# A planner that may hold a transpose back, and power-of-two scales in three vector operations

## The chip, the cores and the metric

The kernel runs on one core of one Trainium2 chip. The metric is the device time of one execution in microseconds (us), from its start to its end. Three executions of the kernel before took 875.47, 883.95 and 887.24 us, so the median is 883.95. A fourth one was profiled, and all rows below are from it.

The engines of the core are TensorE (PE in the rows, PEld for its loading of weights), VectorE (DVE), ScalarE (ACT), GpSimd (POOL) and SyncE (SP), which issues the transfers. Each engine works through its instructions strictly in the order in which the program lists them, and waits on semaphores for the others.

## The reference

Block-sparse attention over q, k and v of 4 batches x 8 heads x 768 rows x 64, followed by a feed-forward layer with a rational activation:

```
mask = |block_i - block_j| <= 1, or block 0 or 23 on either side, or a sampled block (3 for each row block)
attn = softmax(q k^T / 8 where mask) v
x    = attn as 3072 x 512
h    = x @ w_in                                  # 512 x 2048
g    = (a0 + a1 h + a2 h^2 + a3 h^3) / (1 + |b0| |h| + |b1| h^2 + 1e-6)
out  = g @ w_out                                 # 2048 x 512
```

The weights arrive as 64-bit floats and are unpacked on the chip. q, k, x and w_in are scaled by a power of two and split into two 16-bit parts (a high and a low one), so that products of 16-bit matmuls add up to 32-bit precision.

## The kernel before, in words

**Tiling.** The 3072 rows are twelve chunks of 256. A chunk needs eight row blocks of attention (`attention`, one for each batch and block of 32 rows; blocks 0 and 23 have three parts, the others one), which run through scores (L911), maxima (L921), exponentials (L939), a transpose of the probabilities (`turn`, L980), values (L1037); four blocks share one weighting (`weigh`, L1071) and one transpose of x (`turn_x`, L1109), whose result is split into xh (ACT, L150) and xl (DVE, L1125). The feed-forward layer then runs as eight units for each chunk (`unit`): two `into` pieces of 12 matmuls on TensorE (L1179 to L1181), the rational function in three ACT and seven DVE steps besides a logarithm and an exponential, and two `out` pieces of 6 matmuls (L1235 to L1237) into an accumulator.

**Preparation.** For each batch, k is read once for its range (ACT sums absolute values, `bound`, L400) and, after its scale is known, read again, split, transposed on TensorE (`rest`, L683) and written to DRAM. q is loaded by tiles of 128 rows (`prep_q`, L728, into the one buffer ldq), split into hlq (GpSimd high part, L154; DVE low part, L394), transposed (L758), copied by ACT (L762) and swapped by two transfers (L766, L767). Batches 0 and 1 find a scale for each q tile, batches 2 and 3 one for the batch.

**Scales.** `scales` (L343) makes a power of two from a maximum: a transpose on TensorE (`most`, L351) spreads the 128 partition maxima, DVE reduces them (L356), and four short DVE instructions on one column follow: a floor (L359), the exponent by a bit mask (L363), and the scale and its inverse (L367, L368). It is called 27 times: 12 for q tiles (scq), 2 for q batches (scqb), 8 for k and v (sc), 4 for w_in (scw) and once for the x of the first chunk (scx). `prep_q` makes from two inverses the softmax factor c and its negative in three DVE instructions (L746, L749, L752), 14 times.

**Order.** Nothing is ordered by hand. Each step is an `Op` with an engine, a price in ns, its predecessors and a priority. `issue` runs through a clock of its own: for each engine it takes the Op with the smallest key, which is the later of "engine free" and "inputs ready less a slack of 21 ns", then the priority; it writes that Op's instructions and books price and hand-over times (`LAT`). The result is a fixed order on each engine. Up to 80 us of the planner's clock it also writes idle-time matmuls on TensorE (`fill`, L162), whose result nobody uses.

Of the kernel before, what the change touches and what calls it, by code (L numbers as in the profile page):

```python
# [11 lines left out]
F32 = mybir.dt.float32  # L12
# [11 lines left out]
def kernel(  # L24
# [71 lines left out]
    VE, SC, PO, TE, SY = "DVE", "Activation", "Pool", "PE", "SP"  # L96
    LAT = {(SC, TE): 410, (VE, TE): 240, (PO, TE): 225, (TE, SC): 200, (TE, VE): 200, (TE, SY): 170, (VE, SC): 130, (VE, PO): 130,
# [19 lines left out]
    class Op:  # L117


        def __init__(self, eng, price, run, after=(), prio=0.0, takes=(), uses=(), unit=None, behind=None):  # L120
# [3 lines left out]
            self.after, self.behind = [a for a in after if a is not None], behind  # L124
# [3 lines left out]
            self.next, self.at, self.work = [], dict.fromkeys(self.engs, 0.0), 1.0  # L128
# [35 lines left out]
    def issue(ahead):  # L164
# [29 lines left out]
        while left:  # L194
            best = None
            for e, l in todo.items():
                for o in l:
# [7 lines left out]
                    key = (max(t - slack, now[e]) + (0 if e == o.engs[0] else other[e]), o.prio, o.n)  # L205
# [90 lines left out]
    coef = const.tile([P, 4], F32, name="coef")  # L296
    bias = const.tile([P, NB, NS], F32, name="bias")
# [6 lines left out]
    def setup():  # L304
# [5 lines left out]
        nc.vector.memset(coef[:, 0:1], 1.0)  # L310
        nc.vector.tensor_copy(out=coef[:, 1:2], in_=absb[:, 0:1])
# [31 lines left out]
    def scales(get, name, after, prio, slot=(), finish=None, keep=None):  # L343
# [14 lines left out]
        def floor():  # L358
            nc.vector.tensor_scalar(out=res[0][:, 0:1], in0=res[0][:, 0:1], scalar1=2.0 ** -100, scalar2=None, op0=ALU.max)  # L359

        def exponent():
            mi = res[0].bitcast(I32)
            nc.vector.tensor_scalar(out=mi[:, 1:2], in0=mi[:, 0:1], scalar1=0x7F800000, scalar2=None, op0=ALU.bitwise_and)  # L363

        def power():
            m, mi = res[0], res[0].bitcast(I32)
            nc.vector.tensor_scalar(out=mi[:, 2:3], in0=mi[:, 1:2], scalar1=-1.0, scalar2=float((2 * 127 + 14) << 23), op0=ALU.mult, op1=ALU.add)  # L367
            nc.vector.tensor_scalar(out=mi[:, 3:4], in0=mi[:, 1:2], scalar1=float(14 << 23), scalar2=None, op0=ALU.subtract)  # L368
            res[:] = [m[:, 2:3], m[:, 3:4]]
            if keep:  # L370
                keep(*res)
# [4 lines left out]
        a = Op(TE, 109, most, after, prio, takes=[s_ps])  # L376
        a = Op(VE, 260, largest, [a], prio, takes=slot, uses=[s_ps])
        return row(VE, [(69, floor), (69, exponent), (138, power)] + ([(138, final)] if finish else []), [a], prio, uses=slot), res
# [177 lines left out]
    def prep(b, when, what):  # L556
# [11 lines left out]
        for w in what:  # L568
# [40 lines left out]
            if w == 2:  # L609
# [4 lines left out]
                q_scale[b] = scales(lambda mx=mx: mx[0][:, 6:7], "scqb", [o], when(w, 0, n - 1))  # L614
                continue

            def largest(mx=mx, w=w):
# [5 lines left out]
                           finish=out_scale if w and b < PLAIN else None)  # L623
# [14 lines left out]
    def rest(b, w, j, d, o_scale, sc, prio, before):  # L638
# [60 lines left out]
        o = Op(TE, 445, transposes, [o], prio, takes=[s_ps], uses=[s_hl])  # L699
# [13 lines left out]
    def prep_q(b, t, prio, before):  # L713
# [57 lines left out]
        if own:  # L771
            o = Op(SC, 613, most, [o_ld], prio, uses=[s_ld])
            o, sc = scales(lambda: d["mx"][:, 0:1], "scq", [o], prio, sl_sc)
# [634 lines left out]
```

## Time and profile before

| | |
|---|---|
| median of three executions | 883.95 us |
| profiled execution | 879.92 us, its span from first to last instruction 878.2 us |
| TensorE busy | 827.3 us (94%), idle 51 us |
| VectorE busy | 725.5 us (83%) |
| ScalarE busy | 675.9 us (77%) |
| GpSimd busy | 112.3 us (13%) |
| transfers | 151 MB, 16 engines 66% busy |

A busy share is an average over stretches that differ, so the rows below go stretch by stretch. In a row of a group the columns are: line, engine, operation, what it writes and reads, count, total busy time, mean ns of one, then the idle time of the engine just before and what ended it. [...]

### The profile page before, as it was taken

The numbers are of one execution on the slowest core, as the hardware profiler recorded it, in microseconds if no ns is written. First come the engines' busy times: TensorE is split into PE (matmuls) and PEld (weight loads), VectorE is DVE, ScalarE is ACT, GpSimd is POOL, SyncE is SP. The second block draws the span as 40 slices with busy tenths as digits, with TensorE's granted clock in tenths as the row PEclk, the third lists the DMA queues.
The fourth block names the chain that finished last, engine by engine and source line by source line (L and its number), as shares of the span: only waits on it lengthen the run. The fifth ranks groups of instructions, "written<-read, shape, count | busy, mean of one in ns | idle before, by whom it ended". The sixth has DMA issues, their size and how long they took to land.

```text
span 878.2 us, 28042 instructions
## 1 busy us (share of the span) xinstructions
PE 827.3 (94%) x10338; PEld 642.6 (73%) x10338; DVE 725.5 (83%) x1746; ACT 675.9 (77%) x1450; POOL 112.3 (13%) x117
## 2 busy tenths in 40 slices
PE   8989868779899899999999999999999899999997
PEld 4456756657678687778878787778778788778886
DVE  6778998999998787787878686888888688778886
ACT  5789988987787788897777687897767587767563
POOL 1146426164300000100000000100000000000000
PEclk9999988998999999999999999999999999999999
DMA  8697799868656966888556956889545965740000
GB/s 195 154 215 224 209 206 202 217 205 215 140 152 169 282 156 175 216 241 229 140 147 177 250 164 172 216 222 242 147 137 160 235 159 155 179 108 26 1 26 24
DMA packets 240216, 151.22 MB, mean 172 GB/s; under 512 B 16208, under 2 KB 222928, under 8 KB 240080
## 3 DMA queue, kind: packets, MB, share of 16 engines
q1 hardware_dynamic: 240080, 149.43, 65.7%
q8 instruction: 82, 1.34, 0.7%
q14 instruction: 54, 0.44, 0.2%
HBM read 132.07 MB, written 11.01 MB: 163 GB/s over the span
## 4 chain that ended last, share of the span: by engine, by line
PE 62%; DVE 11%; DMA 9%; SPq 7%; ACT 6%; issue 3%; POOL 1%; ACTq 0%; POOLq 0%; DVEq 0%
PE acc L1235 8%; PE ph L1179 8%; PE acc L1236 8%; PE acc L1237 8%; PE ph L1180 7%; PE ph L1181 7%; PE av L1037 5%; PE sp L911 4%; PE pt L980 4%; DMA ldq<-in_q_dram 2%; DMA wl<-in_moe_w_in_dram 2%; SPq L1007 1%; DMA vg<-in_v_dram 1%; DMA ld<-in_v_dram 1%; DVE pr L921 1%
## 5 line engine op out<-in xcount | busy, mean ns | idle before, releaser
L1179 PE MATMUL ph<-xh,wi 128*128 128x256 f16 x768 | 214.1, 279 | 4.7 <-DVE tt L1196 3.6
L1181 PE MATMUL ph<-xh,wi 128*128 128x256 f16 x768 | 212.5, 277 | 2.2 <-POOL wi L514 2.2
L1180 PE MATMUL ph<-xl,wi 128*128 128x256 f16 x768 | 212.6, 277 | 0.1
L1235 PE MATMUL acc<-wo_h,gh 128*128 128x512 f32 x376 | 160.8, 428 | 0.0
L1237 PE MATMUL acc<-wo_h,gl 128*128 128x512 f32 x376 | 149.4, 397 | 3.3 <-DVE gl L1224 3.3
L1236 PE MATMUL acc<-wo_l,gh 128*128 128x512 f32 x376 | 149.4, 397 | 0.0
L1203 DVE SCALAR_TENSOR_TENSOR ab<-sq,absb,ab 128x512 f32<-128x512 f32 x96 | 73.4, 764 | 53.4 <-ACT ab L1200 53.3
L1186 ACT ACTIVATE sq<-ph,fc 128x512 f32<-128x512 f32 x96 | 65.8, 685 | 65.9 <-PE ph L1181 65.5
L1179 PEld LDWEIGHTS <-wi 128*128 128x128 f16 x768 | 76.3, 99 | 34.5 <-issue 17.4
L921 DVE CUSTOM_DVE_ANT_1 pr<-sp,bias 128x256 f32<-128x256 f32 x224 | 84.8, 418 | 10.1 <-PE sp L911 10.0
L1214 DVE SCALAR_TENSOR_TENSOR gh<-tt,par,rr 128x512 fp32r<-128x512 f32 x96 | 75.7, 789 | 17.0 <-PE acc L1236 12.2
L939 ACT ACTIVATE pr<-pr,st,cqb 128x256 f32<-128x256 f32 x112 | 66.1, 594 | 29.6 <-DVE st L950 29.4
L1237 PEld LDWEIGHTS acc<-wo_h,gl 128*128 128x128 f32 x376 | 71.0, 189 | 22.2 <-DVE gl L1224 5.1
L1181 PEld LDWEIGHTS <-wi 128*128 128x128 f16 x768 | 76.4, 99 | 12.7 <-POOL wi L514 2.5
L1235 PEld LDWEIGHTS acc<-wo_h,gh 128*128 128x128 f32 x376 | 71.4, 190 | 17.5 <-issue 1.9
L1037 PE MATMUL av<-vg,pT 128*32 128x64 f32 x3584 | 74.4, 224 | 9.5 <-DMA vg<-in_v_dram 5.6
L1180 PEld LDWEIGHTS <-wi 128*128 128x128 f16 x768 | 76.5, 100 | 9.3 <-issue 0.9
L1037 PEld LDWEIGHTS av<-vg,pT 128*32 128x32 f32 x3584 | 56.6, 111 | 34.4 <-issue 11.9
L1236 PEld LDWEIGHTS acc<-wo_l,gh 128*128 128x128 f32 x376 | 71.4, 190 | 11.4
L980 PE MATMUL pt<-ident,pr 128*128 128x128 f32 x448 | 74.8, 288 | 3.3 <-ACT pr L939 3.0
L980 PEld LDWEIGHTS pt<-ident,pr 128*128 128x128 f32 x448 | 67.6, 204 | 13.0 <-ACT pr L939 5.3
L150 ACT ACTIVATE pT<-pt 128x512 f32<-128x512 f32 x112 | 66.5, 593 | 12.5 <-PE pt L980 11.8
(185 smaller groups left out, 1661.0 us busy)
## 6 DMA issues: line engine op xcount, KB each, us to landing
vg<-in_v_dram SPq DMA_DIRECT2D x312, 64.0 KB, 3.1
vg<-in_v_dram SPq DMA_DIRECT2D x88, 192.0 KB, 3.8
vg<-in_v_dram SPq DMA_DIRECT2D x24, 512.0 KB, 5.4
kall<-ks SPq DMA_DIRECT2D x52, 192.0 KB, 3.3
kall<-ks SPq DMA_DIRECT2D x156, 64.0 KB, 2.3
ld<-in_k_dram SPq DMA_DIRECT2D x36, 256.0 KB, 3.5
wl<-in_moe_w_in_dram SPq DMA_DIRECT2D x32, 256.0 KB, 4.9
wl<-in_moe_w_out_dram SPq DMA_DIRECT2D x16, 512.0 KB, 4.3
```

The source lines that it names most:

```text
L150: nc.scalar.activation(out=out, in_=in_, func=AF.Copy, scale=by)
L921: nc.vector.tensor_tensor_reduce(out=prs[x][:, g].rearrange("p (s r) -> p s r", r=BLK), in0=h["sp"][:, g].rearrange("p (s r) -> p s r", r= ...
L980: nc.tensor.transpose(pp[:, jj * P:(jj + 1) * P], cols, ident)
L1037: nc.tensor.matmul(av[rows, g], pT[:, 2 * g + kt, rows] if plain else pT[:, 2 * g + kt, pa_, rows], vf[:, g * HG + h4, kt * D:(kt + 1) * D ...
L1179: nc.tensor.matmul(o, wh, xh[:, :, cc], start=(cc == 0), stop=False)
L1180: nc.tensor.matmul(o, wh, xl[:, :, cc], start=False, stop=False)
L1181: nc.tensor.matmul(o, wl, xh[:, :, cc], start=False, stop=(cc == NCC - 1))
L1203: nc.vector.scalar_tensor_tensor(out=d["ab"], in0=d["sq"], scalar=absb[:, 1:2], in1=d["ab"], op0=ALU.mult, op1=ALU.add)
L1214: nc.vector.scalar_tensor_tensor(out=d["gh"], in0=d["tt"], scalar=par[:, 0:1], in1=d["rr"], op0=ALU.add, op1=ALU.mult)
L1235: nc.tensor.matmul(acc[:, t], ghs, wo_h[:, f], start=(new and e == 0), stop=False)
L1236: nc.tensor.matmul(acc[:, t], ghs, wo_l[:, f], start=False, stop=False)
L1237: nc.tensor.matmul(acc[:, t], gls, wo_h[:, f], start=False, stop=(last and e == 1))
```

## The change

1. `scales` makes its result in three short DVE instructions in place of four: the inverted exponent in one (xor and mask), a multiplication with a cap (in place of the floor), a reciprocal for the inverse.
2. The softmax factor and its negative come out of one DVE instruction over two columns (a constant tile `signs` holds +SCALE and -SCALE) in place of three.
3. An `Op` may have `late`: 1500 ns that the planner adds to the time at which its inputs are ready. It is set for the transposes of k and q (L683, L758) and for `most` (L351), for batches after the first.
4. An `Op` may have `rush`: 600 ns off its key. It is set for what follows the last attention group of the first chunk: weighting, transpose of x, its scale scx, its split.
5. The transposes of q no longer claim the buffer of the result (`d["slot"]`), the copy behind them does.

```diff
-        def floor():
-            nc.vector.tensor_scalar(out=res[0][:, 0:1], in0=res[0][:, 0:1], scalar1=2.0 ** -100, scalar2=None, op0=ALU.max)
-
-        def exponent():
+        def inverse():
             mi = res[0].bitcast(I32)
-            nc.vector.tensor_scalar(out=mi[:, 1:2], in0=mi[:, 0:1], scalar1=0x7F800000, scalar2=None, op0=ALU.bitwise_and)
+            nc.vector.tensor_scalar(out=mi[:, 1:2], in0=mi[:, 0:1], scalar1=-1, scalar2=0x7F800000, op0=ALU.bitwise_xor, op1=ALU.bitwise_and)
 
         def power():
-            m, mi = res[0], res[0].bitcast(I32)
-            nc.vector.tensor_scalar(out=mi[:, 2:3], in0=mi[:, 1:2], scalar1=-1.0, scalar2=float((2 * 127 + 14) << 23), op0=ALU.mult, op1=ALU.add)
-            nc.vector.tensor_scalar(out=mi[:, 3:4], in0=mi[:, 1:2], scalar1=float(14 << 23), scalar2=None, op0=ALU.subtract)
+            m = res[0]
+            nc.vector.tensor_scalar(out=m[:, 2:3], in0=m[:, 1:2], scalar1=2.0 ** 13, scalar2=cap, op0=ALU.mult, op1=ALU.min)
             res[:] = [m[:, 2:3], m[:, 3:4]]
+
+        def back():
+            nc.vector.reciprocal(out=res[1], in_=res[0])
...
-            nc.vector.scalar_tensor_tensor(out=d["c"], in0=sc[1], scalar=SCALE, in1=kv[b][2], op0=ALU.mult, op1=ALU.mult)
-
-        def factor2():
-            nc.vector.tensor_scalar(out=d["c"], in0=d["c"], scalar1=2.0 ** -64, scalar2=None, op0=ALU.max)
-
-        def factor3():
-            nc.vector.tensor_scalar(out=d["cn"], in0=d["c"], scalar1=-1.0, scalar2=None, op0=ALU.mult)
+            nc.vector.scalar_tensor_tensor(out=d["cc"], in0=signs, scalar=sc[1], in1=kv[b][2].broadcast_to([P, 2]), op0=ALU.mult, op1=ALU.mult)
...
-                    key = (max(t - slack, now[e]) + (0 if e == o.engs[0] else other[e]), o.prio, o.n)
+                    key = (max(t - slack - o.rush, now[e]) + (0 if e == o.engs[0] else other[e]), o.prio, o.n)
...
-                        x.at[y] = max(x.at[y], end + lat)
+                        x.at[y] = max(x.at[y], end + lat + x.late)
...
-        o = Op(TE, 445, transposes, [o], prio, takes=[s_ps], uses=[s_hl])
+        o = Op(TE, 445, transposes, [o], prio, takes=[s_ps], uses=[s_hl], late=0.0 if first else LATE)
...
-        x = Op(TE, 445, transposes, [l], prio, takes=[s_ps, d["slot"]], uses=[s_hl])
-        x = Op(SC, 904, evac, [x], prio, uses=[s_ps, d["slot"]])
+        x = Op(TE, 445, transposes, [l], prio, takes=[s_ps], uses=[s_hl], late=LATE if b else 0.0)
+        x = Op(SC, 904, evac, [x], prio, takes=[d["slot"]], uses=[s_ps])
...
+        for o in plan[first:]:
+            o.rush = 600.0
```

Since the planner writes the order of every engine anew, the whole order shifts a little. In total TensorE gets 11 more idle-time matmuls (210 for 199), DVE 27 instructions fewer from the scales, 28 fewer from the factors and 1 fewer because one `wo_l` (L467) goes to GpSimd, and two small memsets more. All other counts stay but for a few conversions that change between ACT and GpSimd. Three places follow. Line numbers behind L343 are shifted in the changed kernel (L351 is L355, L356 is L360, L683 is L686, L758 is L755).

VectorE at the scale of the first x, before (mx is the maximum of x, scx its scale, scw the scale of weights, xl the low part that the first `into` needs):

```order
L394 SCALAR_TENSOR_TENSOR hlq<-ldq,scq,hlq 128x8x64
L363 TENSOR_SCALAR scw<-scw 128x1
L1094 TENSOR_REDUCE mx<-mx 128x1
L752 TENSOR_SCALAR cq<-cq 128x1
L367 TENSOR_SCALAR scw<-scw 128x1
L368 TENSOR_SCALAR scw<-scw 128x1
L497 COPY wscale<-scw 128x1 x2
L356 TENSOR_REDUCE scx<-sp 128x1
L359 TENSOR_SCALAR scx<-scx 128x1
L363 TENSOR_SCALAR scx<-scx 128x1
L367 TENSOR_SCALAR scx<-scx 128x1
L368 TENSOR_SCALAR scx<-scx 128x1
```

And with the change:

```order
L1068 TENSOR_TENSOR xn<-av,sm 128x512
L496 TENSOR_REDUCE sums<-sums 128x1
L360 TENSOR_REDUCE scq<-sp 128x1
L1092 TENSOR_REDUCE mx<-mx 128x1
L360 TENSOR_REDUCE scx<-sp 128x1
L364 TENSOR_SCALAR scx<-scx 128x1
L368 TENSOR_SCALAR scx<-scx 128x1
L372 RECIPROCAL scx<-scx 128x1
L1095 COPY xs_1101<-scx 128x1
L360 TENSOR_REDUCE scw<-sp 128x1
```

Between the weighting xn (L1071, now L1068) and the maximum of x stood twelve instructions, the split of hlq the last but one of them; now two stand there, and the other scales come after scx. On ACT the order moves likewise: three copies kx (L863) stood ahead of the range of x and now stand behind it, and the copy qa (L762) no longer stands ahead of xh.

TensorE at the transpose of the fourth q tile of batch 3 (at 688.86 us in the trace; hlq is the split tile, wi the weights of `into`, pt the transposed probabilities), before:

```order
L1180 LDWEIGHTS wi
L1180 MATMUL ph<-xl_120,wi 128x256
L1181 LDWEIGHTS wi
L1181 MATMUL ph<-xh_119,wi 128x256
L1037 MATMUL av<-vg_110,pT 32x64 x16
L758 LDWEIGHTS hlq
L758 MATMUL sp<-ident_96,hlq 128x128
```

And with the change:

```order
L1235 MATMUL acc<-wo_h,gh 128x512
L1236 MATMUL acc<-wo_l,gh 128x512
L1237 MATMUL acc<-wo_h,gl 128x512
L977 MATMUL pt<-ident,pr 128x128 x4
L755 LDWEIGHTS hlq
L755 MATMUL sp<-ident_96,hlq 128x128
```

The transpose now stands one score, one `into` and one values step earlier in TensorE's list. At the q tiles of 489.12 and 547.98 us in the trace it stands behind the same work as before. SP issues the loads of these tiles behind the same transfers of keys and values as before (one 512 KB transfer fewer at 489).

SP at the reading of k for batch 2 (L595 reads for the range, L548 reads again for the split), before, at 346 to 352 us in the trace:

```order
L883 DMA kall<-ks 128x256
L595 DMA ld<-in_k_dram 128x512
L548 DMA ld<-in_k_dram 128x4x128 x3
L1001 DMA vg_112<-in_v_dram 48x8x128
L1007 REGISTER_ALU
```

And with the change:

```order
L598 DMA ld<-in_q_dram 128x512
L598 DMA ld<-in_k_dram 128x512 x2
L873 DMA kall<-ks 128x8x256
L996 DMA vg_111<-in_v_dram 128x8x128
L598 DMA ld<-in_k_dram 128x512 x2
L551 DMA ld<-in_k_dram 128x4x128 x3
L875 DMA xkg_4276<-ks 128x3x256
```

Three reads for the range and three for the split, 256 KB each, move up by 51 to 69 of SP's 997 transfers, to among the three-part loads that stand at 288 to 300 us in the trace.

## Rows read from the trace of the kernel before

**Rows 1.** Three stretches of the span: start:end and length in us, then busy us and count of each engine, the granted clock, the busy share of the transfer engines and GB/s.

```profile
44.00:88.00 44.00, 40.79 (x680) 25.84 (x680) 35.74 (x115) 40.48 (x105) 23.81 (x24) 1.00 0.90 219
88.00:242.00 154.00, 127.69 (x1828) 98.71 (x1820) 148.89 (x358) 132.25 (x301) 60.55 (x54) 0.93 0.82 199
242.00:878.00 636.00, 619.44 (x7449) 497.77 (x7438) 511.14 (x1169) 472.65 (x974) 19.25 (x23) 0.99 0.61 162
```

**Rows 2.** TensorE's groups of the steps that get `late`, first three from 120 to 300 us, then three from 300 us to the end.

```profile
L683 PE MATMUL sp<-ident,hl 128*128 128x128 f16 x48 | 3.7, 220 | 2.1 <-ACT kt L150 1.9 <-DVE st L921 0.2
L758 PE MATMUL sp<-ident,hlq 128*128 128x128 f16 x33 | 2.7, 220 | 1.7 <-DVE cq L749 1.4 <-DVE xscale L607 0.3
...
L351 PE MATMUL sp<-ident,mx 128*128 128x128 f32 x2 | 0.6, 284 | 0.3 <-DVE scq L359 0.3
...
L758 PE MATMUL sp<-ident,hlq 128*128 128x128 f16 x120 | 9.7, 226 | 5.5 <-DVE hlq L394 5.5
L683 PE MATMUL sp<-ident,hl 128*128 128x128 f16 x96 | 7.4, 220 | 1.5 <-DVE hl L394 0.6 <-DVE st L921 0.6 <-ACT kt L150 0.3
L351 PE MATMUL sp<-ident,mx 128*128 128x128 f32 x6 | 1.8, 293 | 1.1 <-DVE mx L618 0.8 <-DVE st L950 0.3
```

**Rows 3.** The timeline: start, length, engine, line, operation, and in brackets the idle time before. First TensorE's transposes of two q tiles, then the latest of these waits: SP's issue, TensorE's first matmul of one `into` and the values behind it, then GpSimd, DVE and the transpose.

```profile
489.12 0.62 PE L758 MATMUL sp<-ident,hlq 128*128 128x128 f16 x8 [1.81 <-DVE hlq L394]
...
547.98 0.62 PE L758 MATMUL sp<-ident,hlq 128*128 128x128 f16 x8 [1.46 <-DVE hlq L394]
...
679.88 2.22 SPq L728 DMA_DIRECT2D ldq<-in_q_dram  x2
...
684.57 0.28 PE L1179 MATMUL ph<-xh,wi 128*128 128x256 f16 x1
...
685.99 0.65 PE L1037 MATMUL av<-vg,pT 128*32 128x64 f32 x32
...
687.33 0.69 POOL L154 TENSOR_SCALAR hlq<-ldq,scqb 128x512 f16<-128x512 f32 x1 [37.12 <-DMA ldq<-in_q_dram]
...
688.06 0.75 DVE L394 SCALAR_TENSOR_TENSOR hlq<-ldq,scqb,hlq 128x512 f16<-128x512 f32 x1 [4.53 <-POOL hlq L154]
...
688.86 1.04 PE L758 MATMUL sp<-ident,hlq 128*128 128x128 f16 x8 [2.22 <-DVE hlq L394]
```

**Rows 4.** Short stretches at 488 and 688 us, columns as in rows 1.

```profile
488.00:492.00 4.00, 2.88 (x34) 2.14 (x35) 3.69 (x6) 2.21 (x4) 0.28 (x1) 0.82 1.17 304
492.00:496.00 4.00, 4.00 (x65) 2.75 (x63) 2.47 (x9) 3.28 (x9) 0.00 (x0) 0.75 1.09 317
...
688.00:692.00 4.00, 3.14 (x19) 2.51 (x20) 3.94 (x10) 1.06 (x3) 0.02 (x1) 0.57 1.11 260
```

**Rows 5.** How often the floor of the scales (L359, first row) and the second step of the factors (L749, second row) run from 88 to 242 us: busy us and count on DVE, then clock and transfers.

```profile
88.00:242.00 154.00, 1.15 (x8) 0.93 0.82 199
...
88.00:242.00 154.00, 0.58 (x4) 0.93 0.82 199
```

**Rows 6.** DVE's timeline where two scales run among other work.

```profile
225.29 0.14 DVE L359 TENSOR_SCALAR sc<-sc 128x1 f32<-128x1 f32 x1
225.35 0.14 DVE L367 TENSOR_SCALAR scq<-scq 128x1 int32<-128x1 int32 x1
225.41 0.14 DVE L368 TENSOR_SCALAR scq<-scq 128x1 int32<-128x1 int32 x1
```

**Rows 7.** Groups: the `wo_l` step on DVE and on GpSimd, and the nearest rows to a one-column reciprocal.

```profile
L467 DVE TENSOR_TENSOR wo_l<-dw,wo_h 128x512 fp32r<-128x512 f32 x1 | 0.7, 693 | 0.5 <-ACT wo_h L150 0.5
...
L467 POOL TENSOR_TENSOR wo_l<-dw,wo_h 128x512 fp32r<-128x512 f32 x15 | 22.9, 1527 | 14.4 <-ACT wo_h L150 13.7
...
L1064 DVE TENSOR_SCALAR sm<-sm 128x8 f32<-128x8 f32 x24 | 4.9, 204 | 2.6 <-ACT pr L939 2.3
L1067 DVE RECIPROCAL sm<-sm 128x8 f32<-128x8 f32 x24 | 4.8, 199 | 0.4
```

**Rows 8.** The timelines of ACT, DVE and TensorE from the weighting of the first chunk's last group to the first `into`.

```profile
65.17 1.00 ACT L863 COPY kx<-kall 128x256 f16 x3
66.08 0.58 ACT L400 ACTIVATE scrap<-ph 128x512 f16<-128x512 f32 x1
...
68.85 1.30 ACT L762 ACTIVATE qa<-sp 128x1024 f16<-128x1024 f16 x1
...
63.56 0.69 DVE L1071 TENSOR_TENSOR xn<-av,sm 128x512 f32<-128x512 f32 x1 [0.39 <-PE av L1037]
...
66.14 0.75 DVE L394 SCALAR_TENSOR_TENSOR hlq<-ldq,scq,hlq 128x512 f16<-128x512 f32 x1
...
70.72 1.41 DVE L1125 SCALAR_TENSOR_TENSOR xl<-ph,xs,xh 128x512 f16<-128x512 f32 x2 [1.43 <-ACT xh L150]
...
71.84 0.27 PE L1179 MATMUL ph<-xh,wi 128*128 128x256 f16 x1
```

**Rows 9.** Groups of TensorE from 352 to 364 us that wait for batch 2's k.

```profile
L683 PE MATMUL sp<-ident,hl 128*128 128x128 f16 x24 | 1.8, 219 | 0.9 <-DVE hl L394 0.6 <-ACT kt L150 0.3
...
L351 PE MATMUL sp<-ident,mx 128*128 128x128 f32 x1 | 0.3, 323 | 0.8 <-DVE mx L618 0.8
```

**Rows 10.** Columns as in rows 1: the three-part loads before batch 2.

```profile
290.00:296.00 6.00, 3.40 (x42) 2.23 (x45) 3.03 (x7) 6.00 (x16) 0.00 (x0) 1.00 1.11 329
```

**Rows 11.** A run of 20 idle-time matmuls in TensorE's timeline.

```profile
67.52 4.48 PE L162 MATMUL acc<-ident 128*128 128x512 f16 x20
```

More of the change, by code (lines that the diff above doesn't have):

```diff
@@ L117, with __init__ @@
     class Op:
-        def __init__(self, eng, price, run, after=(), prio=0.0, takes=(), uses=(), unit=None, behind=None):
+        def __init__(self, eng, price, run, after=(), prio=0.0, takes=(), uses=(), unit=None, behind=None, late=0.0):
             self.alt = eng if isinstance(eng, dict) else None
@@ L123, in __init__ @@
             self.eng, self.price, self.run, self.prio, self.unit = self.engs[0], price, run, prio, unit
-            self.after, self.behind = [a for a in after if a is not None], behind
+            self.after, self.behind, self.rush = [a for a in after if a is not None], behind, 0.0
             self.takes, self.uses = list(takes), list(takes) + list(uses)
@@ L127, in __init__ @@
                 s.left += 1
-            self.next, self.at, self.work = [], dict.fromkeys(self.engs, 0.0), 1.0
+            self.next, self.at, self.work, self.late = [], dict.fromkeys(self.engs, 0.0), 1.0, late
             plan.append(self)
@@ L296 @@
     coef = const.tile([P, 4], F32, name="coef")
+    signs = const.tile([P, 2], F32, name="signs")
     bias = const.tile([P, NB, NS], F32, name="bias")
@@ L340, with scales @@
     o_setup = Op(VE, 5300, setup, [o_small], prio=-70, uses=[s_work])
-    def scales(get, name, after, prio, slot=(), finish=None, keep=None):
+    def scales(get, name, after, prio, slot=(), finish=None, keep=None, late=0.0, cap=2.0 ** 114):
         res, d = [], {}
@@ L374, in final @@
             finish(*res)
-        a = Op(TE, 109, most, after, prio, takes=[s_ps])
+        a = Op(TE, 109, most, after, prio, takes=[s_ps], late=late)
         a = Op(VE, 260, largest, [a], prio, takes=slot, uses=[s_ps])
-        return row(VE, [(69, floor), (69, exponent), (138, power)] + ([(138, final)] if finish else []), [a], prio, uses=slot), res
+        return row(VE, [(69, inverse), (69, power), (75, back)] + ([(138, final)] if finish else []), [a], prio, uses=slot), res
     def split16(ld, s, hl, w, eng):
@@ L613, in prep @@
                 o = Op(VE, 75, largest, los, when(w, 0, n - 1))
-                q_scale[b] = scales(lambda mx=mx: mx[0][:, 6:7], "scqb", [o], when(w, 0, n - 1))
+                q_scale[b] = scales(lambda mx=mx: mx[0][:, 6:7], "scqb", [o], when(w, 0, n - 1), late=LATE, cap=2.0 ** 40)
                 continue
@@ L772, in prep_q @@
             o = Op(SC, 613, most, [o_ld], prio, uses=[s_ld])
-            o, sc = scales(lambda: d["mx"][:, 0:1], "scq", [o], prio, sl_sc)
+            o, sc = scales(lambda: d["mx"][:, 0:1], "scq", [o], prio, sl_sc, late=LATE if b else 0.0, cap=2.0 ** 40)
         else:
@@ L778, in prep_q @@
         if own or t == 0:
-            d["oc"] = row(VE, [(70, factor), (69, factor2), (69, factor3)], [o, k_scale[b]], prio, takes=d["cslot"], uses=sl_sc)
+            d["oc"] = row(VE, [(70, factor)], [o, k_scale[b]], prio, takes=d["cslot"], uses=sl_sc)
             d["first"] = d
@@ L1077, in attention @@
         G["ops"] = [Op(VE, 600, weigh, [o for o in G["ops"] if o.eng == TE] + [oinv], p, takes=[G["s_xn"]], uses=G["av"] + [G["s_sm"]])]
+        first = len(plan) - 1
         if c:
```

5 lines of the change are left out of this document (4 added, 1 removed).

## The prediction

> **What bounds the kernel now.** I read the stretches first [rows 1], since the shares over the whole span mix two regimes. From 242 us on, TensorE is busy 619.4 of 636 us: it is the bound there, and only its 16.6 us of idle time and its moments at half clock can be won. From 88 to 242 us VectorE is busy 148.9 of 154 us while TensorE is idle for 26.3 us: VectorE is the bound, and a wait of TensorE that goes away there brings nothing by itself. Before 88 us ACT (40.5 of 44 us) and the chain of first results set the pace, and TensorE fills its time with matmuls that nobody uses [rows 11].
>
> Then I asked what TensorE waits for at the three steps that get `late` [rows 2]. Up to 300 us that is 2.1 + 1.7 + 0.3 = 4.1 us, all within VectorE's stretch. Behind 300 us it is 5.5 + 1.5 + 1.1 = 8.1 us, and there it counts. The largest is 2.22 us at the q tile of 688.86 us [rows 3]: its load was issued at 679.88 us, GpSimd could start at 687.33, DVE at 688.06, and TensorE stood before a transpose that the planner had put too early. [...]
>
> **The change part by part.**
>
> *Short DVE instructions.* 27 go with the scales and 28 with the factors. Each is about 0.145 us long, but between other work the next one starts 0.06 us later [rows 6]: 225.29, 225.35, 225.41. So one that is taken out of a full queue gives back 0.06 us. In VectorE's stretch 8 scales and 4 factors run [rows 5]; that is 8 x 1 + 4 x 2 = 16 instructions, 1.0 us. One `wo_l` leaves DVE (0.69 us long, 0.6 from start to start), and goes to GpSimd for 1.5 us [rows 7], which has 93 us free in that stretch [rows 1]. Together 1.6 us less on the engine that is the bound, and I count all of it. The other 39 lie where DVE has slack: 0. A one-column reciprocal isn't in the trace; at eight columns it takes 199 ns where the nearest other instruction takes 204 [rows 7], so I price it like the instruction that it replaces. The bounds are 0 (all of it hidden) and 16 x 0.145 + 0.69 = 3.0 us.
>
> [...]
>
> *The first scale with `rush`.* From the weighting at 63.56 us to the first `into` at 71.84 us the chain takes 8.3 us [rows 8]. In its way stand three copies kx on ACT (1.0 us, ahead of the range of x at 66.08), the split of hlq on DVE (0.75 us, ahead of the maximum) and the copy qa on ACT (1.3 us less 0.1 of overlap, ahead of xh, on which xl waits). The new order has all three behind the step that they delayed, so the first `into` should come 2.5 to 3 us earlier. What of it reaches the end? ACT is 92% busy there and has the same work, and the moved copies are now late for the second chunk's scores. What can be won is what the late chain cost VectorE: it idled 1.43 us before xl [rows 8], and its work is the bound soon after. I take 1.5 us, with 0 and 3.0 as ends.
>
> *`late` at the transposes.* It only helps where the order really changes. For the k of batch 2, the loads have moved up by 51 to 69 places on SP, so what TensorE waited for, 0.8 + 0.6 + 0.3 us [rows 9], should be there: 1.7 us won. At 489.12 and 547.98 us the transpose stands behind the same work as before, and its load behind the same transfers but for one: 0, the waits stay, and the half clock with them. At 688.86 us the transpose stands even earlier, by one `into` (685.99 - 684.57 = 1.4 us), one values step (0.65 us) and one score (about half an `into`, 0.6 us), with the load where it was [rows 3]. Then TensorE stops up to 2.6 us longer. As the load may also come earlier with everything ahead of it, I book 1.0 us of loss, with 0 and 2.6 as ends. A transpose that comes later could make the next scores late. It can't here: from a q transpose to the first score of its tile lie at least 8 us of TensorE's own work in either order, counted piece by piece with an `into` at 1.4 us [rows 3], and 1.5 us more of lead don't use that up.
>
> *The claim on q's result buffer.* It moves from the transpose to the copy behind it. No wait in rows 2 is on that buffer: 0 either way.
>
> *Eleven more idle-time matmuls.* 20 of them take 4.3 us (67.52 to the `into` at 71.84) [rows 8, 11], so 11 take 2.4 us. They are planned into gaps before 80 us, where the pace is set by ACT and DVE: 0, and up to 2.4 us if TensorE runs behind the plan there.
>
> **The sum:** -1.6 - 1.5 - 1.7 + 1.0 = -3.8 us. Against the profiled execution's own 879.92 us that gives 876.1. The median of the three runs, 883.95, lies 4.0 us higher, and the mean of all four executions is 881.6, which would give 877.8. I forecast **877 us**, no change that can be measured: 2% of 884 us is 17.7 us, about what a measurement of this kernel can tell from none.
>
> **The rivals.**
>
> *All waits close.* The planner leaves 1.5 us more before each of the late transposes; if loads and ACT come as it thinks, the 8.1 us behind 300 us go, and with them the half clock (3.4 us). With 1.6 us from DVE and 3.0 from the first scale that is 16.1 us: 863.8 against the profiled run, 864. For it speaks that TensorE is the bound there and every us counts in full. Against it, that at three of the four largest waits the order of TensorE and SP is as it was, or the wrong way. Chance 0.17, and 0.13 that it passes the 2%.
>
> *The pulled-up reads push the keys and values back.* Six reads of 256 KB are now in SP's queue among the three-part loads, where the transfer engines are full already (share 1.11, 329 GB/s [rows 10]). 1.57 MB at 329 GB/s are 4.8 us by which keys and values of the next blocks land later. Once the lead of those loads (two or three buffers) is used up, TensorE waits at scores and values instead. This decides if the lead at 300 us is under 4.8 us; TensorE idled 2.6 of 6 us in that place already [rows 10], which says that the lead is thin. With the 2.6 us at 688 us and 2.4 us of idle-time matmuls, less the 1.6 us of DVE: 879.9 + 8.2 = 888, slower than before. Chance 0.14, and 0.05 that the same at batch 3 brings it beyond 2%.
>
> *Nothing of it arrives.* The changed order is another draw of much the same plan, `late` binds nowhere, and the first chunk's lead is spent before 88 us ends: 880 to 884. Chance 0.09.
>
> **How the numbers follow.** The forecast with its bounds has the remaining 0.60: its ends are 3.0 + 3.0 + 1.7 = 7.7 us better (872) and 2.6 + 2.4 us worse than the profiled run (885), and runs of one kernel spread from 875 to 887. For 8 in 10 I reach to the first rival's 864 and to just past the second's 888: 863 to 890. Faster by over 2%: 0.13 and 0.03 from the forecast's own spread, 0.16. Slower by over 2%: 0.05 and 0.01, 0.06. Within: 0.78.
>
> **What would show it.** DVE's short instructions: the same 0.06 us from start to start, and the reciprocal no longer than 0.16 us. The first scale: the first `into` near 69 us, and DVE's 1.4 us gap before xl gone. The k of batch 2: no wait at its range and its first transpose. The q tiles of batches 2 and 3: waits of 1 to 4 us on hlq that are still there, with the half clock behind them; if they are gone, the first rival is right. Scores and values that wait for transfers near 300 us speak for the second. The prediction is wrong altogether if VectorE's stretch ends more than 5 us earlier or later than 242 us with the same work, since then the order within that stretch, which I hold to be neutral, was what counted.

## The result, and the profile after

The changed kernel takes 891.3 us (median of 12 runs, 889.1 to 897.9), the kernel before 880.1 (12 runs, 875.5 to 887.2) on the same chip: a ratio of 1.0128, 95% interval 1.0094 to 1.0162. It is slower, by 1.3%, inside the 2% that I called no change and just above my range.

The head of the page of the changed kernel and its first queue: busy us, share of the span and count per engine; for the queue packets, MB, and the time of its packets as a share of 16 engines' span.

```profile
span 889.3 us, 28038 instructions
...
PE 828.2 (93%) x10349; PEld 645.7 (73%) x10349; DVE 728.8 (82%) x1692; ACT 676.1 (76%) x1452; POOL 113.6 (13%) x116
...
q1 hardware_dynamic: 240080, 149.43, 67.6%
```

The same work (TensorE was busy 827.3 us before), and 10 us more of idle time (61.1 us for 50.9). DVE lost 54 instructions and is busy 3.3 us longer. And the queue: before, the same 240080 packets and 149.43 MB took 65.7% of 878.2 us, 577 us of each transfer engine; now 67.6% of 889.3, **601 us**.

In a row of a stretch the granted clock is a mean share of full speed; single records in the traces of the two kernels have it at 1.00 or at 0.50 and nowhere between. The stretches of [rows 1] in the changed kernel, and TensorE's waits from 300 us on (total, times, longest):

```profile
88.00:242.00 154.00, 124.52 (x1871) 96.62 (x1863) 148.55 (x343) 130.87 (x303) 62.74 (x56) 0.92 0.84 198
...
242.00:878.00 636.00, 618.10 (x7486) 499.12 (x7486) 510.20 (x1152) 477.20 (x984) 17.27 (x22) 0.99 0.64 161
```
```profile
PE av L1034 <- ACT pT L151: 10.3, 6, 5.9
PE pt L977 <- ACT pr L936: 2.3, 1, 2.3
PE sp L755 <- DVE hlq L397: 1.4, 1, 1.4
```

The three waits for hlq of [rows 2, 3] (5.5 us) have shrunk to one of 1.4, at the tile of 688.86 us, which now comes at 696.60. In their place the values wait for pT, once for 5.9 us. Where the loss arises is read best from how late a given step comes: the first matmul of the 1st, 9th, 33rd, 89th, 93rd and 189th `into`, taken from the two traces, less the kernel before (the kernels below the first line are those of the experiments):

| us late at `into` no. (time before) | 1 (72) | 9 (133) | 33 (246) | 89 (473) | 93 (490) | 189 (854) |
|---|---|---|---|---|---|---|
| changed kernel | -2.5 | 8.6 | 6.4 | 6.0 | 12.5 | 11.0 |
| e5: before, all tiles 32 bytes on | -1.3 | -0.8 | -0.9 | 1.4 | 3.6 | 7.1 |
| e6: changed, tiles in their old places | -3.7 | 8.2 | 5.5 | 7.2 | 12.2 | 8.5 |
| e7: order of before, old places, short scales | -1.6 | -1.2 | -1.6 | -1.8 | -0.7 | -3.3 |
| e8: as e6 without the lead | -0.9 | 4.2 | 0.8 | 2.2 | 2.0 | 2.0 |
| e9: as e6 without `late` | -2.4 | 12.7 | 3.6 | 4.2 | 3.8 | -0.1 |
| e12: as e6, three rows moved near 490 us | -3.3 | 12.4 | 8.3 | 9.1 | 9.6 | 8.4 |
| e14: before, load targets at multiples of 512 bytes | -1.9 | -1.4 | -1.6 | -4.1 | -4.3 | -6.7 |

Each line is one execution, and at the end executions of one kernel lie up to 12 us apart (875.5 to 887.2 us for the kernel before), so differences of a few us between two lines show nothing by themselves; the ratios of many runs below decide. The changed kernel loses about 6 us up to 246 us, in VectorE's stretch (on the way it is 14.2 us late at the 13th `into` and 3.3 at the 29th), and about 6 us at 490.

**Near 490 us**, first DVE's split in the kernel before, then timelines of SP, DVE, ACT and TensorE in the changed kernel, and last its stretches behind the stop (columns as in [rows 1]):

```profile
488.31 0.75 DVE L394 SCALAR_TENSOR_TENSOR hlq<-ldq,scqb,hlq 128x512 f16<-128x512 f32 x1 [4.45 <-POOL hlq L154]
...
483.87 1.38 SPq L731 DMA_DIRECT2D ldq<-in_q_dram  x2
485.31 2.47 SPq L598 DMA_DIRECT2D ld<-in_q_dram  x2
...
491.32 0.75 DVE L397 SCALAR_TENSOR_TENSOR hlq<-ldq,scqb,hlq 128x512 f16<-128x512 f32 x1 [8.29 <-POOL hlq L155]
...
484.23 0.69 ACT L151 ACTIVATE xh<-sp,xscale 128x512 f16<-128x512 f32 x1
490.84 0.63 ACT L403 ACTIVATE scrap<-ld 128x512 f16<-128x512 f32 x1 [5.92 <-DMA ld<-in_q_dram]
...
493.30 0.58 ACT L151 ACTIVATE pT<-pt 128x512 f32<-128x512 f32 x1
...
493.93 1.08 PE L1034 MATMUL av<-vg,pT 128*32 128x64 f32 x32 [5.90 <-ACT pT L151]
...
492.00:496.00 4.00, 2.07 (x38) 1.59 (x39) 4.00 (x11) 2.72 (x6) 0.00 (x0) 0.58 1.17 228
496.00:500.00 4.00, 4.00 (x15) 3.14 (x14) 2.85 (x6) 3.47 (x10) 0.00 (x0) 0.56 1.17 251
```

q's tile 15 is issued at 483.87. DVE has reached its split by 483.0 and stands there for 8.3 us, in which no later step of its list starts; before the change it stood there too, for 4.45 us, but the split came one unit of the feed-forward layer and one xl later in its list. ACT stands before the range of a q block whose load was issued behind that one; before the change it stood before no load there. The denominator's steps on DVE and pT on ACT wait behind them, and TensorE behind those. `late` held back TensorE's transpose of the tile. Nothing held back the split ahead of it. Behind the stop the granted clock is 0.58 and 0.56 over 4 us each (the trace has it at 0.50 from 492.67 to 499.49 us), where it was 0.82 and 0.75 [rows 4] (at 0.50 from 490.57 to 493.98). An estimate of the work lost, the missing share times 4 us, is (0.42 + 0.44) x 4 = 3.4 us for (0.18 + 0.25) x 4 = 1.7.

**Up to 246 us.** DVE has no more work there than before, but single instructions are long. DVE's timeline, and GpSimd's beside it:

```profile
183.27 1.13 DVE L947 TENSOR_SCALAR st<-st,cq 128x2 f32<-128x2 f32 x1
...
230.06 1.17 DVE L947 TENSOR_SCALAR st<-st,cq 128x2 f32<-128x2 f32 x1
231.14 0.14 DVE L368 TENSOR_SCALAR scq<-scq 128x1 f32<-128x1 f32 x1
...
183.15 2.87 POOL L517 TENSOR_TENSOR wi<-dw,wi 128x512 f16<-128x512 f32 x2 [1.27 <-ACT wi L151]
...
229.55 1.65 POOL L470 TENSOR_TENSOR wo_l<-dw,wo_h 128x512 fp32r<-128x512 f32 x1 [1.29 <-ACT wo_h L151]
```

An instruction that takes 0.22 us elsewhere takes 1.2 us, until GpSimd's ends (229.55 + 1.65 = 231.2). From 88 us to the 33rd `into` I added up, for each DVE instruction more than 0.1 us longer than the median of its line and shape, the excess: about 19 us before, about 24 after, and each of these instructions overlaps one of GpSimd's. With idle time (5.1 and 6.6 us) that is some 6 us more, nearly the step's whole lag (252.5 - 246.2 us). This is a sum read from two traces; no run takes GpSimd's work away and keeps the order.

### The profile page after: what moved, and what is told of

It is laid out like the page before. It is cut to its first block, busy times and chain, and to the rows that moved or that the text cites. A ratio compares the mean times of both kernels' runs of the same rounds, so it can differ in the third digit from the quotient of the medians.

```text
span 889.3 us, 28038 instructions
## 1 busy us (share of the span) xinstructions
PE 828.2 (93%) x10349; PEld 645.7 (73%) x10349; DVE 728.8 (82%) x1692; ACT 676.1 (76%) x1452; POOL 113.6 (13%) x116
## 2 busy tenths in 40 slices
DMA packets 240215, 151.21 MB, mean 170 GB/s; under 512 B 16208, under 2 KB 222928, under 8 KB 240080
## 3 DMA queue, kind: packets, MB, share of 16 engines
q1 hardware_dynamic: 240080, 149.43, 67.6%
## 4 chain that ended last, share of the span: by engine, by line
PE 59%; DVE 15%; DMA 10%; ACT 7%; SPq 5%; issue 4%; POOL 0%; ACTq 0%; POOLq 0%; DVEq 0%
PE acc L1235 8%; PE ph L1179 8%; PE acc L1236 7%; PE acc L1237 7%; PE ph L1180 7%; PE ph L1181 7%; PE av L1034 5%; PE pt L977 4%; PE sp L908 4%; DMA vg<-in_v_dram 3%; DMA ld<-in_v_dram 2%; DMA ldq<-in_q_dram 2%; ACT pr L936 2%; DVE pr L918 2%; SPq L1004 1%
## 5 line engine op out<-in xcount | busy, mean ns | idle before, releaser
L1179 PE MATMUL ph<-xh,wi 128*128 128x256 f16 x768 | 211.7, 276 | 2.0 <-DVE tt L1196 2.0
L1180 PE MATMUL ph<-xl,wi 128*128 128x256 f16 x768 | 210.4, 274 | 0.0
L1181 PE MATMUL ph<-xh,wi 128*128 128x256 f16 x768 | 210.4, 274 | 0.0
L1179 PEld LDWEIGHTS <-wi 128*128 128x128 f16 x768 | 75.4, 98 | 30.4 <-issue 17.5
L1034 PE MATMUL av<-vg,pT 128*32 128x64 f32 x3584 | 76.3, 228 | 18.0 <-ACT pT L151 14.4
L977 PE MATMUL pt<-ident,pr 128*128 128x128 f32 x448 | 77.6, 294 | 8.5 <-ACT pr L936 5.2
L1235 PEld LDWEIGHTS acc<-wo_h,gh 128*128 128x128 f32 x376 | 72.0, 191 | 16.9 <-issue 2.6
L1180 PEld LDWEIGHTS <-wi 128*128 128x128 f16 x768 | 75.6, 98 | 9.5 <-issue 1.7
L1181 PEld LDWEIGHTS <-wi 128*128 128x128 f16 x768 | 75.5, 98 | 9.2
L1220 DVE SCALAR_TENSOR_TENSOR tt<-tt,par,ab 128x512 f32<-128x512 f32 x96 | 74.4, 775 | 0.9
```

The source lines that it names most:

```text
L977: nc.tensor.transpose(pp[:, jj * P:(jj + 1) * P], cols, ident)
L1034: nc.tensor.matmul(av[rows, g], pT[:, 2 * g + kt, rows] if plain else pT[:, 2 * g + kt, pa_, rows], vf[:, g * HG + h4, kt * D:(kt + 1) * D ...
L1179: nc.tensor.matmul(o, wh, xh[:, :, cc], start=(cc == 0), stop=False)
L1180: nc.tensor.matmul(o, wh, xl[:, :, cc], start=False, stop=False)
L1181: nc.tensor.matmul(o, wl, xh[:, :, cc], start=False, stop=(cc == NCC - 1))
L1220: nc.vector.scalar_tensor_tensor(out=d["tt"], in0=d["tt"], scalar=par[:, 0:1], in1=d["ab"], op0=ALU.add, op1=ALU.subtract)
```

## The experiments

All ratios are to the kernel before on the same chip, with 95% intervals. The first theories: A, lead and `late` each cost about 6 us, early and at 490; B, `late` costs both; C, any redrawn plan lands elsewhere.

**Numbers to zero** (e1 `late`, e2 the lead, e3 both), and **e4**, in which a list of the kernel before's choices replaces the planner's, so that only the arithmetic changes:

```diff
-    LATE = 1500.0
+    LATE = 0.0
...
-            o.rush = 600.0
+            o.rush = 0.0
...
+            o = plan[ORDER[len(plan) - left]]
```

e1: 

> The changed kernel with the 1.5 us of `late` set to 0; the lead of the first scale, the short scales and the moved claim stay. Theory A (two separate losses: the lead of the first scale costs about 6 us before 250 us, `late` costs about 5 us at 484 to 494 us): 885 to 887 us, the 33rd `into` step (246 us in the kernel before) 5 to 8 us late as in the changed kernel, no stop of TensorE over 3 us near 490 us. Theory B (`late` causes both losses): 878 to 881 us, the 33rd `into` within 1.5 us of the kernel before. Theory C (any change of the planner's numbers draws another plan, and no part is to blame): a loss or gain of up to 6 us at some third place, with no relation to either part.

e2: 

> The changed kernel with the lead of the first scale set to 0; `late`, the short scales and the moved claim stay. Theory A: the early 6 us are gone (33rd `into` within 1.5 us of the kernel before), the stop near 490 us is still there: 884 to 886 us. Theory B: 889 to 892 us, as the changed kernel. Theory C: anything from 875 to 890 us, with the stops in other places.

e3: 

> The changed kernel with both numbers at 0, so only the short scales and factors and the moved claim are left, and the planner draws its order anew from their prices. Theories A and B: 877 to 880 us. Theory C: as far from 880 us as the other two, in either direction (up to 6 us), since the redrawing alone does it.

e4: 

> The short scales and factors and the moved claim, but every engine in the recorded order of the kernel before (the planner's choice is replaced by the list of its choices, with two steps of each factor left out). This prices the arithmetic without any change of order. My prediction: 1.6 us faster (0 to 3.0), so a ratio of 0.998 (0.9966 to 1.0). If the last reciprocal or the two-column product is longer than the instructions that it replaces: 0 to 2 us slower.

Measured: e1 1.0059 (1.0029 to 1.0089), e2 1.0056 (1.0026 to 1.0087), e3 1.0119 (1.0061 to 1.0176), e4 **1.0076** (1.0045 to 1.0107). Taking both numbers away is no better than keeping both: A and B fall (e2 alone would fit A, with its 33rd `into` 0.8 us late). And e4 keeps the order and is slower all the same. Its short instructions don't explain that, since its 33rd `into` comes 0.3 us late; its losses begin behind 276 us, the largest where TensorE waits for hlq (4.6 us at 496 and 3.3 at 700), and its packets took 66.8% of 890.2 us, 595 us.

**The tile `signs`.** The built programs give the places (bytes from the start of a partition):

```
             before   changed, e1 to e4, e5   e11      e13      e14
vg0          114816   114848                  114880   114944   114688
first ld     180736   180768                  180800   180864   180736
vg0 mod 256     128      160                     192        0        0
```

The diff's one new constant of two columns takes 32 bytes ahead of every tile that a load writes, par excepted. Theory D: that shift costs. e5 is the kernel before and this:

```diff
+    unused = const.tile([P, 2], F32, name="unused")
     bias = const.tile([P, NB, NS], F32, name="bias")
```

e6 to e8 keep the constants in two free columns of absb instead, so that no tile moves; e6 is otherwise the changed kernel, e7 is e4, e8 is e2:

```diff
-    absb = const.tile([P, 2], F32, name="absb")
+    absb = const.tile([P, 4], F32, name="absb")
...
-    signs = const.tile([P, 2], F32, name="signs")
+    signs = absb[:, 2:4]
```

e5: 

> The kernel before with nothing changed but one unused tile of two columns in the place where the change puts its tile `signs`. The allocator rounds it to 32 bytes, so every tile behind it, the targets of all loads among them, lies 32 bytes further in SBUF. Theory D (the new tile alone slows the transfers, since their targets were multiples of 64 bytes and now aren't): 886 to 890 us, the time of the queue's packets at least 66.5% of the span in place of 65.7%, the waits for hlq near 490 and 700 us longer, as in the run with the order of before. Theory E (the addresses don't matter, the short instructions made that run slower): 880 to 883 us and 65.7%.

e6: 

> The changed kernel, with its two constants in two unused columns of the tile absb, so that every tile lies where it lay before the change. Order and arithmetic are those of the changed kernel. Theory D: about 6.5 us off the changed kernel's time (what the run with the order of before lost), 883 to 886 us; the 33rd `into` step still 3 to 6 us later than before the change, since that part is the order; the stop near 490 us shorter than 3 us. Theory E: 891 us, as the changed kernel.

e7: 

> The short scales and factors in the recorded order of the kernel before, with the constants in absb, so neither order nor addresses differ from before. Theory D: 880 us less the 1.6 us of my prediction (0 to 3.0), a ratio of 0.9966 to 1.0. Theory E: 888 us again.

e8: 

> The changed kernel without the lead of the first scale (set to 0) and with the constants in absb; `late`, the short scales and the moved claim stay. Theory D with a loss of order that comes from the lead: 878 to 881 us, the 33rd `into` step within 1.5 us of the kernel before. Theory E: 886.5 us, as the same kernel with the tile of its own.

Measured: e5 **1.0049** (1.0016 to 1.0082), e6 1.0080 (1.0049 to 1.0112), e7 1.0005 (0.9970 to 1.0040), e8 0.9974 (0.9948 to 1.0000). D holds: the shift alone costs 0.5%, and taking it back gains 0.7% between e4 and e7, 0.8% between e2 and e8, 0.5% between the changed kernel and e6. (The order of e3, measured again at the old places below, gains only 0.1%, with intervals of 0.5% on both sides.) The queue in e5 and e7, same columns as above:

```profile
span 885.3 us, 28043 instructions
...
q1 hardware_dynamic: 240080, 149.43, 67.0%
```
```profile
span 874.8 us, 27991 instructions
...
q1 hardware_dynamic: 240080, 149.43, 65.9%
```

That is 593 and 577 us for the same packets. The interval of e7 holds both the gain of 1.6 us that I had predicted and none. TensorE pays at the hlq steps, the 5.5 us of [rows 2] in the kernel before; first e5, then e14 of the next part:

```profile
L760 PE MATMUL sp<-ident,hlq 128*128 128x128 f16 x120 | 10.1, 232 | 9.3 <-DVE hlq L396 9.3
```
```profile
L758 PE MATMUL sp<-ident,hlq 128*128 128x128 f16 x112 | 8.7, 221 | 4.2 <-DVE hlq L394 4.2
```

From the 33rd to the 189th `into` TensorE is idle for 16.9 us in e5 and 12.0 before, and its mean granted clock is 0.989 and 0.994, 3.4 us of work by the same estimate; together these are the 8 us that e5 loses there.

e6 is half wrong: I expected a short stop at 490 us and 883 to 886 us; the stop was 5.6 us, and 0.8% of the loss is still there.

**Which places the transfers want.** e11 and e13 are e5 with an unused tile of 64 and 128 bytes; e14 takes 128 bytes of constants out of the way:

```diff
-    par = const.tile([P, 8], F32, name="par")
+    par = p2.tile([P, 8], F32, name="par", bufs=1)
...
```

e11: 

> The kernel before with an unused tile of 64 bytes in the place where the run with 32 bytes had its own; nothing else differs from that run. If a multiple of 64 bytes is what the transfers want: 879 to 882 us and 575 to 579 us of 16 engines' time for the queue's packets, as before. If any shift costs, or a multiple of 128 is wanted: 884 to 888 us and over 585 us.

e13: 

> The kernel before with an unused tile of 128 bytes in the same place; nothing else differs from the runs with 32 and 64 bytes. In the kernel before every load's target lies at a multiple of 128 bytes. If that is what the transfers want: 879 to 883 us and 574 to 581 us of 16 engines' time for the queue's packets, as in the runs with the tiles in their old places. If a larger multiple counts, or if the mere presence of another tile costs: 885 to 888 us and over 585 us.

e14: 

> The kernel before with four small constants (128 bytes in all) taken from the pool at the start and put behind the pairs of work tiles, so that kall, the three vg, ldq and kt lie at multiples of 512 bytes in place of 128; ld, qc and the rest stay. If the packets gain from a multiple of more than 128 bytes: under 570 us of 16 engines' time, and 874 to 878 us. If 128 is enough: 574 to 581 us and 879 to 883 us.

Measured: e11 1.0077 (1.0045 to 1.0109) and 593 us of packet time, as e5; e13 0.9961 (0.9921 to 1.0001) and 61.8% of 878.8, **543 us**; e14 **0.9923** (0.9880 to 0.9967) and 61.9% of 871.0, 539 us. Neither of my cases for e13 came: its packet time wasn't as before but better (of the time, the interval still touches 1), since 128 bytes bring kall, the vg and ldq from odd multiples of 128 to multiples of 256 (and ld from a multiple of 512 to an odd one of 128). The kernel before stood badly itself. e14 came out faster than the 874 to 878 us that I expected, but not by its transfers alone: the weights of `out` moved too, and TensorE's matmuls that read them got shorter (34.1 us for 34.7 in 144 of them, last section). By place of these tiles the packets took 593 to 601 us (multiples of 32 or 64 bytes; six traces), 574 to 581 (odd multiples of 128; eight) and 539 to 547 (of 256 or 512; five), whatever the order.

**The order.** At the places of before, with the short scales, all four draws of lead and `late` now stand side by side: F, the lead alone costs; G, each number draws another plan. e9 and e10 are e6 with `late` at 0 and with both at 0, e15 is the kernel before with one number without purpose changed:

```diff
-    MARGIN = 17.0
+    MARGIN = 16.0
```

e9: 

> The changed kernel with the constants in absb and `late` at 0; the lead of the first scale stays. Theory F (the lead alone costs the order's 7 us): 886 to 889 us. Theory G (the plan is redrawn by every number; lead and `late` don't add, and the same order in the shifted layout came to 1.0059, of which the shift is 0.0049): 880 to 883 us.

e10: 

> The changed kernel with the constants in absb and both the lead and `late` at 0: only the prices of the short scales and factors redraw the plan. Theory F: 878 to 881 us, since neither the lead nor `late` is there. Theory G: 885 to 889 us, since the same order came to 1.0119 in the shifted layout, less 0.0049 for the shift.

e15: 

> The kernel before with one number of its planner, the margin behind each step, at 16 in place of 17 ns: a new draw of the order that serves no purpose; arithmetic and places stay. Theory G (each draw lands within about 1% of another, whatever was meant): a ratio between 0.993 and 1.010, and differing from 1 by more than 0.3% is as likely as not, with TensorE's stops in other places. Theory F (only the lead costs): 879 to 883 us.

| | lead | no lead |
|---|---|---|
| `late` | 1.0080 (e6) | 0.9974 (e8) |
| no `late` | 1.0005 (e9) | 1.0105 (e10) |

Measured: e9 1.0005 (0.9979 to 1.0031), e10 1.0105 (1.0057 to 1.0152), e15 0.9972 (0.9946 to 0.9998). Beside `late` the lead costs 1.1%; without it, it gains 1.0%. Neither has a price of its own: G (e10 lies just beyond the 889 us that I gave it). DVE's held time up to the 33rd `into` is about 16 us in e8, 17 in e15 and 22 in e6, so part of the spread may be which of DVE's steps fall beside GpSimd's; I read that from traces and tried it in no run of its own. It isn't all: e9, with no more held time than the kernel before (about 19 us), is 3.6 us late there. An early lag isn't the end's either: e9 is 3.6 us late at 246 us and on time at the end, e10 2.0 and 7.7.

**The stop at 490 us.** e12 replays e6's order with the split moved behind six steps of DVE (nine instructions) and a range read of ACT behind pT (of the two reads that the expectation names, only one changes its place). In DVE's list:

```diff
-hlq<-ldq,scqb,hlq
 ab<-sq,absb,ab
...
+hlq<-ldq,scqb,hlq
 ab<-ab,gh
```

> The changed kernel with the constants in absb and its recorded order, with three rows moved near 490 us: the split of q's tile 15 on DVE goes behind six instructions that now stand behind it, and two reads of ranges on ACT go behind the copy pT that now stands behind them. TensorE, GpSimd and SP keep their order. Theory H (TensorE's stop of 5.6 us there is DVE and ACT standing in order before transfers that the planner thought had landed): the stop is under 2 us and the time 883 to 886 us. If TensorE then stops at the next scores or at the transposes of that tile for as long: 887 to 889 us.

Measured: 1.0060 (1.0030 to 1.0091), 887.3 us. TensorE's longest stop there is 1.9 us (5.6 in e6), and from the 89th to the 93rd `into` it loses 0.5 us (5.0): H holds for the place. ACT's rows in e12:

```profile
489.22 0.60 ACT L251 ACTIVATE pT<-pt 128x512 f32<-128x512 f32 x1 [0.66 <-PE pt L1052]
489.71 0.62 ACT L1285 ACTIVATE rr<-rr 128x512 f32<-128x512 f32 x1
493.09 0.63 ACT L478 ACTIVATE scrap<-ld 128x512 f16<-128x512 f32 x1 [2.75 <-DMA ld<-in_q_dram]
```

But the total gained 0.2%, not 0.5%, and the intervals of 0.3% on either side can't tell that from nothing: that the stop costs the kernel its 5 us is not shown. Behind it e6 wins 3.7 us back (12.2 to 8.5), e12 1.2. From the 93rd to the 189th `into` e12's TensorE is idle for 0.7 us more and its mean granted clock is 0.995 against 1.000, 1.7 us of work by the same estimate; whether that follows from the missing stop, two single executions don't tell.

**Together.** e16 is e8 with e14's places; e17 and e18 are e6 and e8 with the targets of all loads but par's at multiples of 512 bytes.

e16: 

> The changed kernel without the lead, constants in absb, and the small constants moved as in the run above. The kernel without the lead came to 0.9974 of before; if multiples of 512 bytes help, 0.990 to 0.995 (874 to 878 us); if 128 is enough, 878 to 882 us.

e17: 

> The changed kernel with lead and `late` as they are, constants in absb, and par, absb, coef and wscale put ahead of the ld tiles, so that every tile that a load writes, save par itself, lies at a multiple of 512 bytes. If its order costs the same in this layout (1.008 to 0.9974 in the old one): 1.1% over the run beside it, 876 to 880 us. If part of that loss was TensorE's stop near 490 us behind a late load, which faster packets shorten: 870 to 875 us.

e18: 

> The same layout with the lead of the first scale at 0 (`late`, short scales and moved claim stay). Against the run with kall, vg, ldq and kt alone at multiples of 512 (0.9866 of before, 543 us of packet time) the targets of the copies to qc and of the first k loads are new at multiples of 512: 535 to 543 us and a ratio of 0.983 to 0.989, 866 to 871 us. It would beat both kernels. If the two-way spread of orders takes it back: 872 to 878 us.

Measured: e16 **0.9866** (0.9825 to 0.9907; 870.1 us), e17 0.9984 (0.9949 to 1.0018; 879.5 us), e18 0.9897 (0.9867 to 0.9927; 871.4 us); packets 543, 547 and 540 us. The order costs 0.9% here too (e17 to e18), so order and place come near to adding up. e16 is better than I expected, e18 a little worse. e16 and e18 beat both kernels; which of the two is better their intervals don't tell.

## Why the prediction was wrong

My 877 us was -3.8 us on the profiled run; measured is +1.3%, some 11 us. By its steps:

- **What the change adds.** The step that failed first is one that isn't there: I costed every instruction of the diff and let the tile `signs` pass, though the diff shows it. Its 32 bytes cost 0.5% (e5), about 4 us.
- **The order in VectorE's stretch, "which I hold neutral".** It was not, and this is the larger failure: with the tiles in their old places the change still costs 0.8% (e6), about 7 us. The 33rd `into` is 6.4 us late, beyond the 5 us that I had named as the sign for this. I took DVE's work there as a fixed sum. By the traces it isn't one, since an instruction beside GpSimd's takes up to 1 us more, and each order puts other ones there. That the order costs the time is shown by e6, e8, e9 and e10; that it does so through these instructions is argued.
- **Short instructions, -1.6.** The count is right (54 fewer, with two memsets and the `wo_l`), and the 0.06 us between the removed ones too; but I priced what replaces them wrongly. DVE's groups of the two new operations, last number mean ns:

```profile
L749 DVE SCALAR_TENSOR_TENSOR cq<-signs,scq,sc 128x2 f32<-128x2 f32 x12 | 4.0, 332 | 0.0
L372 DVE RECIPROCAL scq<-scq 128x1 f32<-128x1 f32 x12 | 1.9, 155 | 0.1
```

  The reciprocal keeps to my 0.16 us. The two-column product takes 0.22 us in the median where its one-column form took 0.15 (the means, 332 and 219 ns, hold four and two instructions of over 0.5 us, all beside one of GpSimd's); in a full queue the next start comes 0.13 us behind it, not 0.07 (median of the trace). A factor so gives back 0.07 us and not 0.12, and the stretch at most 0.7 us and not 1.0. In e7, where nothing else differs (the `wo_l` stays on DVE), its length from the 1st to the 33rd `into` is unchanged to 0.1 us, and the kernel is at 1.0005, with an interval that can't tell 0.7 us from 1.6.
- **The first scale, -1.5.** The first `into` came 2.5 us earlier, as forecast; DVE's gap before xl halved (1.43 to 0.87 us). What I booked at the end didn't come: 61 us later the lag is 8.6 us.
- **k of batch 2, -1.7.** Its waits are gone [rows 9], as forecast, but at 366.74 us the turn waits 2.3 us for pr, shortly after ACT stood for 3.4 us before the range of a v block, and one transpose waits 0.8 us for kt at 380.3. Nothing won.
- **The q tiles, +1.0.** Wrong on all three. The transpose of 548 us doesn't wait any more; that of 689 us waits 1.4 us, less than its 2.2 and not more, and the half clock behind it is gone (1.00 from 696 to 700 us); at 490 us, where I had 0, is the largest stop. I looked at what TensorE's row moved past, and not at the split and the range reads, which wait for the same load on other queues.

The rivals: "all waits close" was right that the waits for hlq would shrink (5.5 to 1.4 us) and wrong that the time would follow; that `late` shrinks them isn't shown, since e8, which has it, waits 1.7 and 3.8 us for hlq near 491 and 691 us, and e9, which hasn't, 1.5 us once. The 3.4 us that this rival books for the half clock are no time that a run shows: they are my estimate from the clock of [rows 4], the missing share times the length, (0.18 + 0.25 + 0.43) x 4. Counted in the same way, the changed kernel lacks 3.4 us behind its stop at 490 us and none from 696 to 700 us. The pulled-up reads did no harm near 300 us (lag 8.4 us at 276, 5.7 at 310); their like, in batch 3, stood at 490 us. "Another draw of much the same plan" was the right kind, and its 880 to 884 us far too narrow: four draws of the same arithmetic at the same places span 0.9974 to 1.0105. I had runs of one kernel for the spread, and none of one plan.

## What to carry to other kernels

A new tile is a change to every address behind it (here by 32 bytes): read where the targets of loads lie before and after, and try them at multiples of 256 bytes or more (539 to 547 us of packet time here, 593 to 601 at multiples of 32 or 64); the step from 32 bytes off to the best places (e5 to e14, about 1.3%, some of it TensorE's own) was worth as much as the whole spread of orders. Where a planner sets the order, measure a redraw without purpose first; an edit that gains less than that spread has not been shown to do anything. A lead for one engine's step did nothing here for the steps ahead of it that wait for the same load in other queues: DVE stood 8.3 us before the split of the tile near 490 us.

## What the runs showed of the hardware that I had not expected

**Places of load targets.** The same 240080 packets took 593 to 601, 574 to 581 or 539 to 547 us of 16 engines' time with most targets at multiples of 32 or 64, odd multiples of 128, or multiples of 256 bytes and more. With vg0 at 0, 128, 160 and 192 bytes behind a multiple of 256 (e14, the kernel before, e5 and e11) it was 539, 577, 593 and 593 us. Why the place counts was not shown. Not tried was which of the tiles matter, and the shorter packet time of e13 alone gave no gain in time that is clear of noise.

**DVE beside GpSimd.** 48 instructions st<-st,cq average 272 ns before and 341 after; three of them were over 0.4 us before, eight after, all while GpSimd worked. In the rows near 230 us above, DVE's 1.17 us end at 231.23 us and GpSimd's `wo_l` at 231.20. What ties the two together was not shown.

**Where a matmul's operand lies.** In e14 the lead over the kernel before also grows from 6.1 us at 784 us to 6.7 at 854, where the transfer engines are nearly idle (7% busy before). The traces say where: the `out` matmuls, whose operands wo_h and wo_l moved to multiples of 512 bytes. One of their groups from 780 to 850 us, before and in e14 (last number but one mean ns):

```profile
L1236 PE MATMUL acc<-wo_l,gh 128*128 128x512 f32 x47 | 18.7, 398 | 0.0
L1236 PE MATMUL acc<-wo_l,gh 128*128 128x512 f32 x48 | 18.8, 391 | 0.0
```

From the 165th to the 189th `into` TensorE has no idle time and the full clock, and takes 69.7 us in the four runs with wo_h and wo_l at multiples of 512 bytes (e14, e16, e17, e18). It takes 70.3 us in the fifteen other traces that I read, with wo_h 96 to 224 bytes behind such a multiple. From start to start the 144 `out` matmuls in it take 34.1 us in e14 and 34.7 before; the `into` matmuls, whose weights wi moved as well, are unchanged. From the 33rd to the 189th `into` that is about 2.4 of the 5.1 us that e14 gains there; the rest is less idle time (at the hlq steps 4.2 us for 5.5) and less half clock (mean granted clock of the whole execution 0.984 for 0.981). Which multiple it takes was not tried.
